# Block-sparse attention and its feed-forward on one core: the opening ordered by head, two score banks, spare matmuls further on, the last output in halves

## The chip, the cores and the metric

The kernel runs on 1 core of one Trainium2 chip. The metric is the device time of one execution in microseconds. The version before took 211.35 us as the median of 8 runs (210.47 to 214.65).

A core has TensorE (PE in the profile, its weight loads PEld), VectorE (DVE), ScalarE (ACT), GpSimd (POOL) and SyncE (SP, which here issues most transfers). Each runs its own instructions in order; semaphores make one wait for another. Matmuls write to PSUM, from which ScalarE and VectorE read.

## The reference

Four batches, 8 heads, 768 positions, head size 64. A block of 32 positions sees its neighbours, the first and the last block, and three drawn blocks; the first and last block see all.

```python
scores = scale * np.matmul(q, k.transpose(0, 1, 3, 2))
...
mask[qb * block:(qb + 1) * block, kb * block:(kb + 1) * block] = True
...
attn = softmax(np.where(mask, scores, -1e9))          # over the last axis
x = (attn @ v).transpose(0, 2, 1, 3).reshape(3072, 512)
h = x @ w_in                                          # 512 -> 1024
solu = h * softmax(h)
ln = (solu - mean(solu)) / np.sqrt(var(solu) + 1e-06) * g_ln
out = ln @ w_out                                      # 1024 -> 512
```

## The kernel before, in words

**Attention.** Heads go in pairs (`pr`, 4 of them), queries in three tiles of 256 (`t`). Keys and queries are turned into `kT` and `qT`, with the head's 64 values in the rows and 24 more rows below: for keys a one-hot of the block, for queries a row of the mask (0 or a large negative number). So one product of 88 rows gives masked scores. A unit (batch, tile, pair) has 12 products of 128 keys by 256 queries (L500), in three score groups of four, `n` = 0 to 2: group 0 is all of the pair's first head, group 1 half and half, group 2 the second head. A score group fills a pair of PSUM banks (`sbank`, three in all), and ScalarE takes its exponential (L511) to `ex`. Three value groups (L521, 8 products each) multiply by `va`, whose last column of ones gives the sum; VectorE divides (L532, L535) into `x`.

**Feed-forward.** For 128 rows at a time: `x` is transposed by a transfer (L565; the first and the last tile on TensorE, L551 and L555), the first product (`hmm`, L576, in four steps of two matmuls) fills a pair of banks, ScalarE takes the exponential with its sum (L585), VectorE multiplies (L589), centres (L593) and takes statistics (L596, L599), GpSimd works out the scale (L601 to L607), the result is transposed (L615 or L551, L555), and the second product (`outp`, L622, four steps) goes to one of two banks `mbank`. The scaled result goes by VectorE (L632) or, in the last three tiles, ScalarE (L635) to `ot`, and by L638 to memory. 24 such half tiles make the output.

**Banks.** Before, pool `sh` holds all three `sbank` pairs and serves the opening's transposes and the scores of batch 0, tiles 0 and 1 (and the last first products). All other scores take `s`, the first two pairs; first products take `h`, the third. The two `mbank` serve transposes, mask products, value sums and second products.

**The opening.** L316 builds masks on GpSimd; L341 transposes the one-hot on TensorE; L345 and L349 copy it out of the same bank on VectorE and ScalarE; L333 and L336 form the block mask, L354 multiplies it out to query rows, L361 copies these. L446 casts the first keys and queries, L464 transposes them, L472 copies them into `kT` and `qT`. L378 and L381 fill the extra columns of `kb` and `qb` for later pairs; L372 makes the latter. Spare matmuls on ones (L683) are written to the third pair of banks ahead of the first score.

**The order.** All work is a list of operations with an engine, an estimated duration, dependencies, pools they take from and a due time. `Plan.run` (L87) places them with a small model of the engines: always the operation that can start earliest, and among those the one that is due first. The tables `A`, `F`, `Q` and `SHIFT` hold due times of units, feed-forward tiles, preparations and kinds of operation. The planned starts only set the order in which each engine's instructions are written, and how many spare matmuls go into a planned gap:

```python
if o.eng == "PE" and o.start <= begin:
    for _ in range(max(0, int((o.start - idle) * SPARE / 0.107))):
        nc.tensor.matmul(flat(sbank[2])[:, 0:P], onesf, onesf, start=True, stop=True)
```

Of the kernel before, what the change touches and what calls it, by code (L numbers as in the profile page):

```python
# [11 lines left out]
ALU = mybir.AluOpType  # L12
# [10 lines left out]
def act_us(n, sbuf=False):  # L23
    return (n + 60 + (52 if sbuf else 0)) / 1200
# [130 lines left out]
def kernel(  # L155
# [33 lines left out]

    SPARE = 1.0  # L190
    NST, NKB, NEX, NX, NE, NSO, NSOT, NXT, NOT = 4, 3, 9, 6, 2, 3, 3, 2, 3
# [82 lines left out]
    def load(b, pr, which, hs=(0, 2)):  # L274
        src, dst, nm = {"k": (k, kst, "kst"), "q": (q, qst, "qst"), "v": (v, vst, "vst")}[which]
        o0 = stage.get((which, b, pr))
        o = op("SP", 0.5, lambda o: nc.sync.dma_start(  # L277
            out=dst[(o0 or o).slot][:, hs[0] : hs[1]].rearrange("p h c d -> p h (c d)"),
            in_=src[b, 2 * pr + hs[0] : 2 * pr + hs[1]].rearrange("h (p c) d -> p h (c d)", p=P)),
            due=-50 + 0.5 * len(loads), take=None if o0 else (nm, "dq") if b else nm,  # L280
            load=LOAD * (hs[1] - hs[0]) / 2, after=loads[-1:])
        if b:
            o.last_of.append((o, "dq"))
            o.held["dq"][0] = 1
        stage.setdefault((which, b, pr), o)
        stage[(which, b, pr, hs[1])] = o
        loads.append(o)
# [27 lines left out]
    def sel(t, us, fill, base, cm, pat, deps, cmp=ALU.is_ge):  # L315
# [3 lines left out]
    ohs = sel(oneh, 0.3, 0.0, 0, NCH, [[1, NCH], [-BLK, NB]], [oh1])  # L319
    ohs = sel(oneh, 0.3, 0.0, BLK - 1, -NCH, [[-1, NCH], [BLK, NB]], [ohs])  # L320
    mids = sel(ident, 0.3, 1.0, 0, 1, [[-1, P]], [mid, ohs], ALU.not_equal)
    io = op("POOL", 0.2, lambda o: nc.gpsimd.iota(kbi, pattern=[[1, NB]], base=0, channel_multiplier=0), [mids],
            due=-2194)

    stat = io
    for args in ((-NEG, 1, -1, [[1, NB]]), (-NEG, 1, 1, [[-1, NB]]), (0.0, -1, 1, [[0, NB]]),
                 (0.0, NB - 2, -1, [[0, NB]])):
        stat = sel(static, 0.16, *args, [stat, stz])
    for c in (0, NB - 1):
# [9 lines left out]
    def selq_tr(o):  # L339
        for c in range(NCH):  # L340
# [3 lines left out]
    sqt = op("PE", NCH * 0.056, selq_tr, [ohs, mids], due=-2190, take="m")  # L344
    sqs = op("DVE", 0.5, lambda o: nc.vector.tensor_copy(out=flat(selq), in_=bank(sqt, BF16)[0:NB, 0:S]), [sqt],  # L345
             due=-2189, last_of=[sqt])


    krow = [op("ACT", 0.7, lambda o: nc.scalar.copy(out=kT[0][D:DM, 0, 0, :], in_=bank(sqt, BF16)[0:NB, 0:S]),  # L349
               [sqt], due=-2189, last_of=[sqt]),  # L350
            op("DVE", 0.37, lambda o: nc.vector.tensor_copy(out=kT[0][D:DM, 0, 1, :], in_=flat(selq)), [sqs],
               due=-2079.6)]
    mps = lambda o: bank(o)[0:NB]
    mmq = [op("PE", (hi - lo) * 0.00043, lambda o, lo=lo, hi=hi: nc.tensor.matmul(  # L354
        mps(o)[:, 0 : hi - lo], maskq, flat(selq)[:, lo:hi], start=True, stop=True), [mq, sqs], due=due, take="m")
        for lo, hi, due in ((0, TW, -2088), (TW, S, -2079))]

    def qrow_op(eng, us, hh, lo, hi, src, deps, due, last_of=()):
        def f(o):
# [4 lines left out]
    qrow = {(0, 0): qrow_op("ACT", 0.38, 0, 0, TW, lambda: mps(mmq[0])[:, 0:TW], mmq[:1], -2087, mmq[:1]),  # L364
            (1, 0): qrow_op("DVE", 0.38, 1, 0, TW, lambda: mps(mmq[0])[:, 0:TW], mmq[:1], -2079.6, mmq[:1]),
            (0, 1): qrow_op("DVE", 0.65, 0, TW, S, lambda: mps(mmq[1])[:, 0 : S - TW], mmq[1:], -2078, mmq[1:])}
    qrow[(1, 1)] = qrow_op("DVE", 0.3, 1, TW, S, lambda: qT[0][D:DM, 0, 0, TW:S], [qrow[(0, 1)]], -2077)
# [44 lines left out]
    def prepare(b, pr, due):  # L412
# [4 lines left out]
        for nm, st, cb, dst in (("k", kst, kb, kT), ("q", qst, qb, qT)):  # L417
# [23 lines left out]
            for part in range(2):  # L441
                due_ = (-2085, -2080)[part] if first else due

                def cast(o, st=st, cb=cb, ld=ld, c0=cas[0] if cas else None, hs=slice(part, part + 1 if first else 2)):
                    d_, s_ = cb[(c0 or o).slot][:, hs, :, 0:D], st[ld.slot][:, hs]
                    (nc.scalar.copy if o.eng == "ACT" else nc.vector.tensor_copy)(out=d_, in_=s_)  # L446

                e = "ACT" if first and nm == "q" else "DVE"
                n = S // 2 if first else S
                if first or not part:  # L450
                    cas.append(op(e, act_us(n, True) + 0.1 if e == "ACT" else dve_us(n, 2), cast,
                                  [stage[(nm, b, pr, part + 1 if first else 2)]], due=due_,
                                  take=None if cas else nm + "b", last_of=[ld], after=cas[:1]))
            ca = cas[0]
            for hh in range(2):
                due_ = (-2085, -2080)[hh] if first else due
                rows = D if first else DM

                where = "sh" if first and hh == 0 else "m"
                at = pair16 if where == "sh" else lambda o: bank(o, BF16)  # L460

# [7 lines left out]
                for lo, hi in ((0, TW), (TW, S)) if first and nm == "q" else ((0, S),):  # L469
                    def cp(o, dst=dst, hh=hh, t=t, rows=rows, lo=lo, hi=hi, at=at):  # L470
# [3 lines left out]
                    e2 = "ACT" if first and nm == "q" and hh == 0 and lo == 0 else "DVE"  # L474
                    x = op(e2, act_us(hi - lo) if e2 == "ACT" else dve_us(hi - lo, 2) + 0.07, cp, [t],
                           due=-2078 if lo else due_ + 0.1, last_of=[t])
                    if first and nm == "q":
# [12 lines left out]
    def attend(b, t, pr, A):  # L490
# [4 lines left out]
        for n in range(3):  # L495
            def score(o, n=n):
                s = sbank[o.slot]
                for m in range(4):
# [4 lines left out]

            so = op("PE", 4 * 0.1087, score, need[0] + (need[1] if n else []), due=A + 0.9 * n,
                    take="sh" if b == 0 and t < 2 else "s")
            last_use.setdefault((b, pr), []).append(so)
# [51 lines left out]
    def feed(b, t, F, by_pe, late):  # L558
# [10 lines left out]
        for a in range(2):  # L569
# [44 lines left out]
            else:  # L614
                st = op("SP", xbar_us(64), lambda o, so=so: nc.sync.dma_start_transpose(  # L615
                    out=sotb[o.slot], in_=sob[so.slot]), [ce] + wo, due=F[a] - 200, take="soT", load=64 * TILE,
                        last_of=[so])
            o0 = None
            for n in range(4):
                def outp(o, n=n, o0=o0, st=st):  # L620
                    for f in (2 * n, 2 * n + 1):
                        nc.tensor.matmul(bank(o0 or o), sotb[st.slot][:, f, :], w_out_sb[:, f, :],  # L622
                                         start=(f == 0), stop=(f == KF - 1))

                om = op("PE", 2 * 0.2156, outp, [st] + wo, due=F[a] + 7 + 0.8 * n, take=None if n else "m",
                        last_of=[st] if n == 3 else [], after=[om_last] if n else [])
                o0 = o0 or om
                om_last = om

            def fin(o, o0=o0, rs=rs):  # L630
                if o.eng == "DVE":
                    nc.vector.tensor_scalar(out=otb[o.slot], in0=bank(o0), scalar1=rsb[rs.slot],  # L632
                                            scalar2=None, op0=ALU.mult)
                else:
                    nc.scalar.activation(out=otb[o.slot], in_=bank(o0), func=ACT.Copy, scale=rsb[rs.slot])  # L635

            fo = op("ACT" if late else "DVE", 0.52 if late else 0.74, fin, [om, rs], due=F[a] + 7, take="ot", last_of=[o0, rs])
            op("SP", 0.45, lambda o, a=a, fo=fo: nc.sync.dma_start(  # L638
                out=out_v[b, 2 * t + a], in_=otb[fo.slot]), [fo], due=F[a], last_of=[fo], load=0.8)

# [3 lines left out]

    A = [51.93, 316.63, -115.93, 231.11, 59.19, -252.77, -562.27, -274.63, -180.24, 25.80, 75.07, -201.10,
         -31.34, -93.78, 23.73, -319.92, -93.53, -52.89, -80.83, -22.04, -376.92, -9.75, 205.17, 275.41,
         -112.76, -464.51, -631.08, -498.27, -7.06, -372.28, 157.83, 217.60, 84.04, 320.33, 507.35, 414.39,
         21.67, -219.75, 54.16, 178.38, -53.69, 42.58, -611.35, 171.75, -151.43, -138.86, 342.15, 543.94]
    F = [-197.56, -107.72, -104.30, -8.09, -3.95, 17.64, 606.07, -83.42, 40.06, 52.29, -182.87, 23.22, -123.31,
         -316.31, -64.31, 252.67, -96.19, 36.13, 1165.15, 493.27, 30.32, 16.50, -322.54, 402.30]  # L650
    Q = [-885.18, -425.71, -91.22, 353.64, 159.27, 116.44, -98.95, 40.67, 1195.36, 573.14, 90.68, 27.21,
         212.02, 207.45, 1374.23, 1441.29]
    for b in range(B):
# [15 lines left out]

    SHIFT = {"score": 83.14, "hmm": 360.52, "outp": 460.27, "pv": -613.9}  # L670
    for o in plan.ops:
# [4 lines left out]

    begin = min(o.start for o in order if o.emit.__name__ == "score")
    idle = m1.seen
    with tc.manual_schedule():
        for o in order:  # L680
            if o.eng == "PE" and o.start <= begin:
                for _ in range(max(0, int((o.start - idle) * SPARE / 0.107))):
                    nc.tensor.matmul(flat(sbank[2])[:, 0:P], onesf, onesf, start=True, stop=True)  # L683
                idle = o.start + o.us * (2 if o.start < COLD else 1)
            o.emit(o)
# [30 lines left out]
```

## Time and profile before

| | |
|---|---|
| median of 8 runs | 211.35 us (210.47 to 214.65) |
| the profiled execution | 210.63 us, span 208.9 us |
| TensorE granted clock, mean | 0.997 |
| exponentials of scores (L511) | 144, 137.6 us busy, 1040 ns each |
| score products (L500) | 576, 82.8 us busy, 272 ns each |
| value products (L521) | 1152, 43.1 us busy, 193 ns each |
| first products (L576) | 192, 51.3 us busy |
| second products (L622) | 192, 47.7 us busy |
| spare matmuls (L683) | 26, 3.1 us busy |

Matmuls overlap, so the mean of one holds its way through the array; the pace is read from start times. ScalarE's exponentials overlap a little too. A group's "idle before" is time in which its engine stood still, with what ended it. "8.61 33.65 ... x36" in a timeline is a row of merged instructions: start, length, number.

### The profile page before, as it was taken

What the parts mean: (1) busy time and instruction counts of PE and PEld (TensorE: products, weight loads), DVE (VectorE), ACT (ScalarE), POOL (GpSimd) and SP (SyncE); (2) the same over time, 40 slices, a digit from 0 to 9 for tenths busy, and PEclk for the clock granted to TensorE, in tenths of its full rate; (3) what the DMA queues carried; (4) which work ended last, traced back from release to release, by engine and by line L of the source; (5) the groups of instructions that cost most, each with busy time, mean ns of one, the idle gap of its engine ahead of it and who ended that gap; (6) DMA issues with size and microseconds to landing.
All of it is one profiled execution on the core that took longest, in us unless ns stands there. A gap on an engine that the chain in (4) does not pass through costs nothing.

```text
span 208.9 us, 5807 instructions
## 1 busy us (share of the span) xinstructions
PE 199.8 (96%) x2298; PEld 141.2 (68%) x2298; DVE 158.1 (76%) x373; ACT 169.9 (81%) x208; POOL 63.0 (30%) x131
## 2 busy tenths in 40 slices
PE   7899998989999999999999999999999999999991
PEld 6689887767769676877776677666676755664540
DVE  3898979849988657767768775988887496889960
ACT  6699999998999999989989689886989837745331
POOL 5143034305631013623325523363210111311140
PEclk9999999999999999999999999999999999999998
DMA  5999998999984186999999999999790464634522
GB/s 171 325 383 349 265 322 176 197 245 261 248 112 111 29 204 226 275 168 292 177 211 234 291 124 320 188 359 202 174 196 3 104 151 110 143 86 118 152 104 100
DMA packets 69120, 41.28 MB, mean 198 GB/s; under 512 B 52189, under 2 KB 64485, under 8 KB 69093
## 3 DMA queue, kind: packets, MB, share of 16 engines
q1 hardware_dynamic: 68496, 39.86, 77.4%
q0 software_dynamic: 544, 1.05, 2.6%
q8 instruction: 18, 0.29, 0.6%
q14 instruction: 10, 0.07, 0.1%
q10 hardware_dynamic: 52, 0.00, 0.0%
HBM read 23.07 MB, written 6.29 MB: 141 GB/s over the span
## 4 chain that ended last, share of the span: by engine, by line
PE 80%; ACT 11%; DVE 3%; DMA 2%; issue 1%; SPq 1%; ACTq 0%
PE sbank L500 25%; PE mbank L622 20%; PE sbank L576 18%; PE mbank L521 14%; ACT ex L511 9%; DMA qst<-in_q_dram 2%; PE mbank L464 2%; PE mbank L551 1%; ACT eso L585 1%; DVE qb L381 1%; SPq L277 1%; DVE eso L589 1%; DVE eso L593 0%; DVE kb L446 0%; DVE kT L432 0%
## 5 line engine op out<-in xcount | busy, mean ns | idle before, releaser
L511 ACT ACTIVATE ex<-sbank 128x1024 bf16<-128x1024 f32 x144 | 137.6, 1040 | 10.4 <-PE sbank L500 9.7
L500 PE MATMUL sbank<-qT,kT 88*128 88x256 bf16 x576 | 82.8, 272 | 2.6 <-ACT ex L511 1.9
L500 PEld LDWEIGHTS <-kT 88*128 88x128 bf16 x576 | 52.5, 97 | 24.2 <-issue 5.7
L576 PE MATMUL sbank<-w_in_sb,xT 128*128 128x512 bf16 x192 | 51.3, 379 | 0.0
L622 PE MATMUL mbank<-w_out_sb,eso 128*128 128x512 bf16 x192 | 47.7, 379 | 0.0
L521 PEld LDWEIGHTS <-ex 128*128 128x128 bf16 x1152 | 41.7, 97 | 5.2 <-issue 0.3
L521 PE MATMUL mbank<-va,ex 128*128 128x65 bf16 x1152 | 43.1, 193 | 0.1
L585 ACT ACTIVATE eso<-sbank 128x1024 bf16<-128x1024 f32 x24 | 24.8, 1033 | 15.0 <-PE sbank L576 10.5
L589 DVE SCALAR_TENSOR_TENSOR eso<-sbank,eso 128x1024 bf16<-128x1024 f32 x24 | 29.3, 1220 | 10.1 <-ACT eso L585 10.0
L596 DVE BATCH_NORM_STATS2 bn<-eso 128x6 f32<-128x512 bf16 x48 | 30.7, 680 | 0.2
L622 PEld LDWEIGHTS <-eso 128*128 128x128 bf16 x192 | 18.4, 98 | 17.1 <-DVE eso L555 0.5
L576 PEld LDWEIGHTS <-xT 128*128 128x128 bf16 x192 | 18.6, 98 | 11.2
L603 POOL TENSOR_SCALAR mv<-se,mv 128x1 f32<-128x1 f32 x24 | 7.2, 300 | 61.3 <-DVE mv L599 52.0
L532 DVE RECIPROCAL r<-mbank 128x4 f32<-128x4 f32 x48 | 8.2, 175 | 20.6 <-PE mbank L521 20.2
L535 DVE TENSOR_TENSOR x<-mbank,r 128x256 bf16<-128x256 f32 x48 | 19.8, 417 | 0.8
L482 POOL CAST va<-vst 128x768 bf16<-128x768 f32 x16 | 13.8, 863 | 17.5 <-DMA vst<-in_v_dram 14.5
L632 DVE TENSOR_SCALAR ot<-mbank,rs 128x512 f32<-128x512 f32 x18 | 13.5, 748 | 4.0 <-PE mbank L622 3.4
L422 POOL CAST kb<-kst 128x768 bf16<-128x768 f32 x12 | 10.4, 863 | 15.9 <-DMA kst<-in_k_dram 15.2
L607 POOL TENSOR_TENSOR rs<-mv,neg_half 128x1 f32<-128x1 f32 x24 | 13.5, 563 | 5.2 <-DVE ot L632 3.9
L601 POOL TENSOR_TENSOR se<-se 128x1 f32<-128x1 f32 x24 | 4.8, 200 | 32.1 <-ACT eso L585 32.1
L593 DVE TENSOR_SCALAR eso<-eso,mu 128x1024 bf16<-128x1024 bf16 x24 | 12.7, 529 | 0.3
L422 POOL CAST qb<-qst 128x768 bf16<-128x768 f32 x12 | 10.1, 839 | 7.5 <-DMA qst<-in_q_dram 3.7
(73 smaller groups left out, 108.4 us busy)
## 6 DMA issues: line engine op xcount, KB each, us to landing
vst<-in_v_dram SPq DMA_DIRECT2D x16, 384.0 KB, 4.4
out_dram<-ot SPq DMA_DIRECT2D x24, 256.0 KB, 2.4
kst<-in_k_dram SPq DMA_DIRECT2D x15, 384.0 KB, 5.3
qst<-in_q_dram SPq DMA_DIRECT2D x15, 384.0 KB, 6.3
w_in_sb<-in_moe_w_in_dram POOLq DMA_DIRECT2D x2, 512.0 KB, 11.3
kT<-in_moe_w_out_dram SPq DMA_DIRECT2D x1, 768.0 KB
qT<-in_moe_w_out_dram SPq DMA_DIRECT2D x1, 768.0 KB, 14.6
eso<-in_moe_w_out_dram SPq DMA_DIRECT2D x1, 512.0 KB
```

What stands on the lines that cost most here:

```text
L422: nc.gpsimd.tensor_copy(out=half(cb[o.slot], 0).rearrange("p (c h d) -> p c h d", c=NCH, h=2), in_=st[ld.slot].rearrange("p h c d -> p c h ...
L482: vc = op("POOL", pool_us(S) + 0.3, lambda o: nc.gpsimd.tensor_copy(out=va[i][:, 2 * pr : 2 * pr + 2, :, 0:D], in_=vst[ld.slot]), [ld, von ...
L500: nc.tensor.matmul(s[:, m, :], kT[i][0:DM, pr, hh, jc * P : (jc + 1) * P], qT[i][0:DM, pr, hh, t * TW : (t + 1) * TW], start=(m % 2 == 0), ...
L511: exs.append(op("ACT", act_us(1024), lambda o, so=so: nc.scalar.activation(out=exb[o.slot], in_=sbank[so.slot], func=ACT.Exp, scale=scale) ...
L521: nc.tensor.matmul(acc[:, qt, hh, :], exb[exs[n].slot][:, m, qt * P : (qt + 1) * P], va[i][:, 2 * pr + hh, jc, :], start=(n + m + qt == 0) ...
L535: nrm = op("DVE", 0.41, lambda o: nc.vector.tensor_tensor(out=xb[x_of[(b, t)].slot][:, :, 2 * pr * D : (2 * pr + 2) * D].rearrange("p a (h ...
L576: nc.tensor.matmul(h[:, f * 512 : (f + 1) * 512], xTb[xp.slot][:, a, c, :], w_in_sb[:, c, f * 512 : (f + 1) * 512], start=(c == 0), stop=( ...
L585: se = op("ACT", act_us(d_ff) + 0.22, lambda o, h0=h0: nc.scalar.activation(out=eb[o.slots["e"]], in_=pair(h0), func=ACT.Exp, accum_out=se ...
L589: so = op("DVE", 1.3, lambda o, h0=h0, se=se: nc.vector.scalar_tensor_tensor(out=sob[o.slot], in0=pair(h0), scalar=1.0, in1=eb[se.slots["e ...
L596: bn = op("DVE", 2 * 0.68, lambda o, so=so: [nc.vector.bn_stats(out=bnb[o.slot][:, f], in_=sob[so.slot][:, f * 512 : (f + 1) * 512]) for f ...
L607: rs = op("POOL", 0.55, lambda o, mv=mv: nc.gpsimd.tensor_tensor(out=rsb[o.slot], in0=mvb[mv.slot][:, 0:1], in1=neg_half, op=ALU.pow), [q2 ...
L622: nc.tensor.matmul(bank(o0 or o), sotb[st.slot][:, f, :], w_out_sb[:, f, :], start=(f == 0), stop=(f == KF - 1))
```

## The change

- The opening's operations get other engines and due times. The one-hot rows go from PSUM to `selq` by ScalarE (not VectorE), and VectorE makes both copies into `kT` from `selq` in SBUF (before: ScalarE from the bank, VectorE from `selq`). The second head's query cast goes to VectorE. The second mask product comes earlier. ScalarE's fills of `kb` come after the first query cast.
- Where two engines copied parts out of one bank, the second now depends on the first (`first_x`, and `qrow[(1, 0)]` on `qrow[(0, 0)]`).
- Scores of batch 0 and the opening's transposes take the two pairs of pool `s`; the third pair is left to spare matmuls until the first product of the feed-forward.
- Spare matmuls go into planned gaps up to the first `hmm` (before: up to the first score), at 0.9 of the gap, counted at 0.0535 us once the planned time is past `COLD`.
- Some estimates in the planner's model change, among them the loads' and GpSimd's.
- The second product of the very last tile is made in two halves of 256 columns, each in its own bank; the first is scaled by VectorE, the second by ScalarE, and each is sent on its own.
- New tables `A`, `F`, `Q`, `SHIFT` (all numbers differ).

Every engine's order from there on is the planner's, and differs through the whole kernel: on TensorE the first scores now go group 0 of tiles 0, 1 and 2, then group 1 of tile 0; value groups often stand one or two at a time between scores; the first feed-forward product stands after 30 score groups (before: after 36). There are 66 spare matmuls (before 26).

```diff
-    SPARE = 1.0
+    SPARE = 0.9
...
-    sqs = op("DVE", 0.5, lambda o: nc.vector.tensor_copy(out=flat(selq), in_=bank(sqt, BF16)[0:NB, 0:S]), [sqt],
+    sqs = op("ACT", 0.75, lambda o: nc.scalar.copy(out=flat(selq), in_=bank(sqt, BF16)[0:NB, 0:S]), [sqt],
              due=-2189, last_of=[sqt])
-    krow = [op("ACT", 0.7, lambda o: nc.scalar.copy(out=kT[0][D:DM, 0, 0, :], in_=bank(sqt, BF16)[0:NB, 0:S]),
-               [sqt], due=-2189, last_of=[sqt]),
-            op("DVE", 0.37, lambda o: nc.vector.tensor_copy(out=kT[0][D:DM, 0, 1, :], in_=flat(selq)), [sqs],
-               due=-2079.6)]
+    krow = [op("DVE", 0.36, lambda o, hh=hh: nc.vector.tensor_copy(out=kT[0][D:DM, 0, hh, :], in_=flat(selq)), [sqs],
+               due=(-2087.5, -2079.8)[hh]) for hh in range(2)]
...
-        for lo, hi, due in ((0, TW, -2088), (TW, S, -2079))]
+        for lo, hi, due in ((0, TW, -2088), (TW, S, -2084.6))]
...
+    qrow[(1, 0)] = qrow_op("DVE", 0.4, 1, 0, TW, lambda: mps(mmq[0])[:, 0:TW], [mmq[0], qrow[(0, 0)]], -2079.6, mmq[:1])
...
-                e = "ACT" if first and nm == "q" else "DVE"
+                e = "ACT" if first and nm == "q" and part == 0 else "DVE"
...
+                    if e == "ACT":
+                        for f in filled["k"]:
+                            plan.follow(f, cas[0])
...
-                where = "sh" if first and hh == 0 else "m"
+                where = "s" if first and hh == 0 else "m"
...
-                    x = op(e2, act_us(hi - lo) if e2 == "ACT" else dve_us(hi - lo, 2) + 0.07, cp, [t],
-                           due=-2078 if lo else due_ + 0.1, last_of=[t])
+                    x = op(e2, act_us(hi - lo) if e2 == "ACT" else dve_us(hi - lo, 2) + 0.07, cp, [t, first_x],
+                           due=due_ + 0.1 + (0.4 if lo else 0), last_of=[t])
+                    first_x = x
...
-                    take="sh" if b == 0 and t < 2 else "s")
+                    take="s")
...
+            w = d_model // 2 if by_pe and late and a else d_model
+            for col in range(0, d_model, w):
...
+                            nc.tensor.matmul(bank(o0 or o)[:, 0:w], sotb[st.slot][:, f, :],
+                                             w_out_sb[:, f, col : col + w], start=(f == 0), stop=(f == KF - 1))
...
+                e = "ACT" if late and not (col == 0 and w < d_model) else "DVE"
...
-    SHIFT = {"score": 83.14, "hmm": 360.52, "outp": 460.27, "pv": -613.9}
+    SHIFT = {"score": -128.51, "hmm": 94.0, "outp": 390.35, "pv": -23.13}
...
-    begin = min(o.start for o in order if o.emit.__name__ == "score")
+    begin = min(o.start for o in order if o.emit.__name__ == "hmm")
...
-                for _ in range(max(0, int((o.start - idle) * SPARE / 0.107))):
+                for _ in range(max(0, int((o.start - idle) * SPARE / (0.107 if o.start < COLD else 0.0535)))):
```

## The prediction

> **What bounds the kernel now.** I read the page first, then the stretches, the two engines' timelines, the opening row by row and the chain of waits at the end.
>
> ```profile
> PE 199.8 (96%) x2298; PEld 141.2 (68%) x2298; DVE 158.1 (76%) x373; ACT 169.9 (81%) x208; POOL 63.0 (30%) x131
> ...
> PEclk9999999999999999999999999999999999999998
> ...
> 8.60:42.50 33.90, 32.48 (x503) 27.71 (x503) 29.43 (x70) 33.52 (x37) 10.22 (x12) 1.00 1.03 283
> 42.50:60.00 17.50, 16.36 (x206) 12.06 (x205) 14.73 (x33) 16.48 (x20) 8.11 (x13) 1.00 1.02 227
> 60.00:186.00 126.00, 125.45 (x1434) 87.25 (x1431) 94.30 (x225) 106.52 (x130) 36.35 (x75) 1.00 0.80 183
> ```
>
> The last three lines are stretches (busy us of PE, PEld, DVE, ACT, POOL, then clock, DMA share, GB/s). Up to 42.5 ScalarE is the full engine (33.52 of 33.90); from 60 on it is TensorE (125.45 of 126). So an opening that is shorter, or exponentials that come faster, bring the end forward only by what TensorE gets done earlier. The granted clock is 1.00 in each stretch.
>
> ```profile
> 8.61 33.65 ACT L511 ACTIVATE ex<-sbank 128x1024 bf16<-128x1024 f32 x36 [1.19 <-PE sbank L500]
> 42.47 1.96 ACT L511 ACTIVATE ex<-sbank 128x1024 bf16<-128x1024 f32 x2 [0.21 <-PE sbank L500]
> ```
>
> 36 exponentials (exps) without a break: (33.65 - 1.02) / 35 = 0.93 us each, against 0.905 when nothing is late (three from 56.71 take 2.85). This is with three score banks. The next view is a later stretch, where the scores have two, as they have in the changed kernel from the start.
>
> ```profile
> 60.42 7.89 ACT L511 ACTIVATE ex<-sbank 128x1024 bf16<-128x1024 f32 x8
> ...
> 62.45 0.60 PE L500 MATMUL sbank<-qT,kT 88*128 88x256 bf16 x4
> 62.88 0.91 PE L521 MATMUL mbank<-va,ex 128*128 128x65 bf16 x24
> 63.63 0.60 PE L500 MATMUL sbank<-qT,kT 88*128 88x256 bf16 x4
> ```
>
> Here the pace is (7.89 - 1.02) / 7 = 0.98. A score group (0.44 us on TensorE by its start times) and a whole triple of value groups (0.75) take 1.18 between two scores, 0.28 more than one exp. With two banks an exp (1.02 until its bank is free), the start of the next score (0.06 to 0.08: 56.81 to 56.87) and score to exp (0.70: 55.09 to 55.79) make 1.80, which is twice 0.90: nothing is left over.
>
> ```profile
> 3.46 0.55 DVE L345 COPY selq<-mbank 24x768 bf16<-24x768 bf16 x1 [0.55 <-PE mbank L341]
> 4.04 0.79 ACT L349 COPY kT<-mbank 24x768 bf16<-24x768 bf16 x1
> 4.85 0.51 ACT L446 CAST qb<-qst 128x384 bf16<-128x384 f32 x1
> 4.86 0.85 PE L464 MATMUL sbank<-ident,kb 128*64 128x128 bf16 x6
> 6.00 0.52 PE L464 MATMUL sbank<-ident,qb 128*64 128x128 bf16 x6
> 7.05 0.36 ACT L472 COPY qT<-sbank 64x256 bf16<-64x256 bf16 x1
> 7.53 0.49 PE L464 MATMUL mbank<-ident,qb 128*64 128x128 bf16 x6 [0.68 <-DVE qT L361]
> ```
>
> The opening. The first score starts at 7.96, right behind the second head's query transposes (7.53), though ScalarE had its inputs ready at 7.41.
>
> ```profile
> 201.90 2.77 PE mbank L622 x12
> 204.67 0.03 ACTq L635
> 204.70 0.05 issue
> 204.75 0.69 ACT ot L635
> ```
>
> The end of the chain: last matmul to 204.67, copy to 205.44, transfer, span 208.9.
>
> **The change, part by part**, against the profiled execution's 210.63 us (0.72 under the median of 211.35; its span is 208.9).
>
> *Opening, first exp.* The copy of the selection rows goes to ScalarE (0.79 there, 3.46 to 4.25), and the 0.79 copy that stood at 4.04 goes to DVE from SBUF (0.35, after it). The query cast then starts at 4.25 to 4.6 (its load's landing is not shown; it was there by 4.85) instead of 4.85. The three mask fills of kb wait behind that cast, on ScalarE, where nothing is due until the query copies. On DVE the key cast comes first, and TensorE has 7 spares ahead of the key transposes and not 13 (1.57 / 13 each), so these start at 4.2 to 4.6, not 4.86. Query transposes: about 5.3, not 6.00. Then ScalarE's two copies (0.36 each) to about 6.9 and the score at 7.1; exp 0.65 later (as 7.96 to 8.61): 7.9, **-0.7**. Bounds -0.3 (the loads land late) and -1.1.
>
> *Opening, exps 2 to 8.* The order by head gives three score groups that need only head 0, but each waits for DVE: key copy 0.55, key cast 0.36, query copy 0.42 (it now waits for ScalarE's copy out of the same bank; the old trace had those in sequence too: 7.41, then 7.51), mask row 0.68. That ends at 8.0. The key transposes of head 1 stand ahead of the second score on TensorE and wait for that mask row's bank: score 8.4, exp 9.1 (before: 9.53). Then on DVE: query cast of head 1 (0.36, moved here from ScalarE), rows 0.42 and 0.28, key copy 0.54, query copy 0.27, cast of the next pair 0.55, query copy 0.41, three mask copies of 0.46 to 12.1; TensorE's transposes for the next pair wait for the last of these (one bank of two). I get exp 8 at 15.1, as before (15.09). So the 0.7 is **given back, +0.7**; bounds 0 and +1.0.
>
> *Exps 9 to 36 on two banks.* Before, from exp 8 to the 37th, 27.4 us. In the changed kernel's order on TensorE, between the 9th and 31st scores, I count between two scores: five whole triples (0.28 each over one exp), triple plus transposes (0.62), two value groups plus transposes (0.37), two transposes (0.20) and three small ones (0.13): 2.7 us. 29 exps at 0.905 are 26.2. One feed-forward exp now comes before the 37th (1.0 on ScalarE); it covers the 0.8 over that I count from the 31st on. 26.2 + 2.7 + 1.0 = 29.9: **+2.5**. Bounds: +0.5 (only the feed-forward exp less half a us) and +3.
>
> *Spares.* 66 against 26; 20 stand ahead of the first score, the other 46 between it and the first feed-forward group, 0.056 each by the rows after 6 us, 2.6 us in all, in runs of at most 6 (0.34). ScalarE sets the pace there; a run stands in a gap that TensorE would wait through. Taken as 0; where a gap isn't there, each run delays a score, at most 2.6. A gain is excluded, as the clock is 1.00 already. The Trainium skill ("TensorE: Matmul & The Clock Gate", Part 1) says that the array's clock falls only after an idle window of some 3.4 us; the longest wait of TensorE after 8 us is 1.03, so by it, too, the spares in the gaps are worth 0, and if it were wrong the trace would show a clock under 1.00 somewhere.
>
> *Work done earlier.* When score 37 starts, the changed kernel has done 5 feed-forward pairs and not 2; all else is equal in number (33 value groups, 16 transposes, 1 x-transpose). 3 pairs of 0.43: **-1.3** off what is left.
>
> *After score 37.* What is left before is 108 scores x 0.436, 111 value groups x 0.25, 94 + 96 pairs x 0.432, 5 transposes x 0.45 = 159.2; it took 204.67 - 41.8 = 162.9, so 3.7 were waits and matmul floors, 1.14 of them between 42.5 and 60. With first products and first outputs 3 to 5 pairs ahead I take these 1.1 as gone: **-1.1**; bounds 0 and -2. Late next would be the transfers: the channel is full (1.02 to 1.03) and SP's order has one xT transpose and the second query transpose earlier, the qst load later. The old kernel's batch-1 rows waited 0.3 on DVE at 40.5; scores are now 2 us later, so 0. GpSimd's order is the same up to there.
>
> *Last output in halves.* 16 matmuls of 256 columns for 8 of 512: 1.74 for 1.73. The copy that ends last is 256 wide: 0.36 for 0.69, -0.33. The transfer is half as big: -0.1 (0 to -0.5: the loads of 192 and 384 KB land in 3.0 and 5.3 us, on a full channel). The second half waits for a bank that DVE reads (0.74) while the first half (0.87) runs: +0.2. **-0.25**. DVE has three sums and statistics in a row there: bounds -0.6, +0.9.
>
> Sum: -0.7 + 0.7 + 2.5 - 1.3 - 1.1 - 0.25 = -0.15: **210.5 us**.
>
> **The rivals.**
> *Faster: the order covers the triples.* If ScalarE runs on two banks as it did on three, the +2.5 shrinks to the 1.0 of the feed-forward exp, and DVE doesn't give the 0.7 back: -0.7 + 1.0 - 1.3 - 1.1 - 0.25 = -2.35, 208.3. For it: steps of 0.90 occur on two banks wherever nothing over 0.47 stands between scores, and here value groups are often single. Against: 0.98 in the fence above.
> *Slower: the lost bank is not made good.* The same +2.5, work in hand -1.3, but none of the 1.1 comes back and DVE holds the last tiles (+0.9): +2.1, 212.7. It decides from an exp pace over 0.98 in the first 36. For it: DVE is 29.43 of 33.90 busy there.
> *Slower: the clock is released later.* Transposes go at 107 ns until 5.5 us and at 56 from 6.08, after spares almost without a gap. With 17 spares and not 26 by then (10 and 7), the release may miss; at 107 the first three scores and four transposes cost 3 x 0.44 + 4 x 0.3, about 2.5 less what waits anyway: +2, 212.6.
> *The change does nothing that lasts:* opening hidden, 210.6; that lies in the forecast's own range.
>
> **How the numbers follow.** Forecast 0.46 (own range 209.0 to 212.2), covered triples 0.31, lost bank 0.15, late clock 0.08. One per cent (2.1 us) is about what a measurement of this kernel can tell from no change. Over 1% faster is most of the second case and the forecast's edge: 0.28; slower the last two: 0.24; within 0.48. The range 208.0 to 213.0 reaches into the cases on both sides.
>
> **What would show it.** First exp near 7.9 with 56 ns transposes from about 6; eighth step near 15; the pace of the first 36 exps 0.99 to 1.02; the 37th score exp near 45; TensorE without a wait over 0.5 from 46 on; the last copy 0.36. Wrong if that pace stays at 0.93 (then 208.3), or if transposes are still at 107 at 7 us.

## The result, and the profile after

The changed kernel takes 210.18 us (median of 24 executions, 209.08 to 214.45) against 211.16 us before (64 executions, 210.04 to 214.65, over all the comparisons). The ratio is 0.9941, interval [0.9927, 0.9956]: 1.2 us less, inside the 1% that the prediction called no change. The forecast of 210.5 was worked out from the old profiled execution: 0.15 less was expected there, and the profiled executions differ by 0.91 (210.63 to 209.72, spans 208.9 and 208.0). A part of the executions of nearly every version here, before and after too, is 3 to 5 us longer and left out of the ratios, so where there were six executions the ratio is to be read and not the median.

By the start times of the two profiled executions:

| mark, us | before | after | difference | predicted |
|---|---|---|---|---|
| first exp | 8.61 | 6.69 | -1.92 | -0.7 |
| 8th exp | 15.09 | 14.12 | -0.97 | 0 |
| 37th score exp | 42.47 | 44.07 | +1.60 | +2.5 |
| last matmul ends | 204.66 | 204.60 | -0.06 | +0.3 |
| last copy ends | 205.43 | 205.24 | -0.20 | 0.0 |
| span | 208.86 | 207.98 | -0.88 | -0.15 |

The steps between the marks say more than the sum: up to the 8th exp the opening brought 1 us that was not forecast, the stretch on two banks cost what was forecast (+2.58), the way from there to the last matmul gave back 1.67 and not 2.2, and the end behind the last matmul 0.8 and not 0.43.

The page of the kernel after, its busy times and the granted clock in 40 slices:

```profile
PE 200.9 (97%) x2346; PEld 144.2 (69%) x2346; DVE 158.2 (76%) x375; ACT 169.7 (82%) x207; POOL 63.3 (30%) x131
...
PEclk9999999999999999999999999999999999999999
```

The stretches of the kernel after, cut where its own first and 37th exps lie (busy us of PE, PEld, DVE, ACT, POOL, clock, DMA share, GB/s):

```profile
6.69:44.07 37.38, 36.44 (x566) 31.77 (x566) 33.43 (x75) 35.55 (x38) 12.08 (x14) 1.00 0.93 277
44.07:60.00 15.93, 15.93 (x176) 11.42 (x175) 13.03 (x32) 14.91 (x19) 7.89 (x13) 1.00 1.14 260
60.00:186.00 126.00, 125.92 (x1468) 88.40 (x1466) 92.80 (x226) 108.42 (x132) 35.56 (x74) 1.00 0.81 183
```

In the first stretch ScalarE is now busy for 35.55 of 37.38 us: 1.8 us of gaps where it had 0.4 of 33.90. TensorE's 36.44 there includes the 46 later spares, so it says little. From 44 on TensorE has no gap left (15.93 of 15.93, 125.92 of 126), where it had 1.14 and 0.55: that part of the forecast holds.

The opening of the kernel after, TensorE's timeline (start, length; "x6" are six matmuls in a row; L341 transposes the one-hot, L695 are spares, L466 the transposes of keys and queries, L503 scores):

```profile
2.33 0.80 PE L341 MATMUL mbank<-ident,oneh 128*24 128x128 bf16 x6
3.06 0.93 PE L695 MATMUL sbank<-onesf 128*128 128x128 bf16 x7
3.91 0.76 PE L466 MATMUL sbank<-ident,kb 128*64 128x128 bf16 x6
4.50 0.50 PE L466 MATMUL sbank<-ident,qb 128*64 128x128 bf16 x6
...
6.06 0.60 PE L503 MATMUL sbank<-qT,kT 88*128 88x256 bf16 x4 [0.36 <-ACT qT L359]
6.88 0.49 PE L466 MATMUL mbank<-ident,kb 128*64 128x128 bf16 x6 [0.22 <-DVE qT L359]
```

The key transposes start 0.95 earlier than the old row at 4.86, the query transposes 1.50 earlier than the one at 6.00, and they already take 0.50 for six: in this execution the pitch of matmuls falls from 107 to 56 ns at about 4.4 us (before: between 5.5 and 6.1). The two last rows hold the waits that hand part of it back: the first score waits 0.36 for ScalarE's copy of head 0's mask row, and the second head's key transposes wait 0.22 for the bank from which VectorE copies the rest of that row.

ScalarE's timeline of the kernel after, at the first exps and at the first one of the feed-forward:

```profile
6.69 1.02 ACT L514 ACTIVATE ex<-sbank 128x1024 bf16<-128x1024 f32 x1 [0.69 <-PE sbank L503]
7.95 8.24 ACT L514 ACTIVATE ex<-sbank 128x1024 bf16<-128x1024 f32 x8 [0.24 <-PE sbank L503]
...
33.47 5.83 ACT L514 ACTIVATE ex<-sbank 128x1024 bf16<-128x1024 f32 x6 [0.49 <-PE sbank L503]
39.45 1.02 ACT L514 ACTIVATE ex<-sbank 128x1024 bf16<-128x1024 f32 x1
40.37 1.02 ACT L588 ACTIVATE eso<-sbank 128x1024 bf16<-128x1024 f32 x1
```

Eight exps in 8.24 us are (8.24 - 1.02) / 7 = 1.03 us each, against 0.93 before; the feed-forward exp at 40.37 (before: 44.32) is the 1.0 us that the prediction put ahead of the 37th.

The end, TensorE's timeline of the kernel after:

```profile
192.38 1.46 PE L629 MATMUL mbank<-w_out_sb,eso 128*128 128x512 bf16 x6
194.61 5.34 PE L629 MATMUL mbank<-w_out_sb,eso 128*128 128x512 bf16 x24 [0.78 <-ACT ot L643]
199.79 0.61 PE L554 MATMUL mbank<-ident,eso 128*128 128x128 bf16 x8
200.78 3.82 PE L629 MATMUL mbank<-w_out_sb,eso 128*128 128x512 bf16 x24 [0.38 <-ACT ot L643]
```

and of the kernel before:

```profile
194.68 1.89 PE L576 MATMUL sbank<-w_in_sb,xT 128*128 128x512 bf16 x8
196.41 0.61 PE L551 MATMUL mbank<-ident,eso 128*128 128x128 bf16 x8
196.85 4.48 PE L622 MATMUL mbank<-w_out_sb,eso 128*128 128x512 bf16 x20
201.30 0.61 PE L551 MATMUL mbank<-ident,eso 128*128 128x128 bf16 x8
201.74 2.92 PE L622 MATMUL mbank<-w_out_sb,eso 128*128 128x512 bf16 x12
```

L629 is the second product (L622 before), L554 the transposes (L551), L643 ScalarE's scaled copy of the output (L635). Before, first products (L576) stood among the last outputs, and no row waits. After, the first products are done by 191.5; what is left all goes through the two `mbank`, and the transposes L554 hold one of them: 0.78 and 0.38 of waits on ScalarE's output copy. The chain of waits of the kernel after ends so:

```profile
203.56 1.05 PE mbank L629 x8
204.61 0.03 ACTq L643
...
204.76 0.47 ACT ot L643
```

The last copy, of 256 columns, takes 0.47; predicted was 0.36.

### The profile page after: what moved, and what is told of

It is laid out like the page before. It is cut to its first block, busy times and chain, and to the rows that moved or that the text cites. A ratio compares the mean times of both kernels' runs of the same rounds, so it can differ in the third digit from the quotient of the medians.

```text
span 208.0 us, 5910 instructions
## 1 busy us (share of the span) xinstructions
PE 200.9 (97%) x2346; PEld 144.2 (69%) x2346; DVE 158.2 (76%) x375; ACT 169.7 (82%) x207; POOL 63.3 (30%) x131
## 4 chain that ended last, share of the span: by engine, by line
PE 86%; ACT 7%; DVE 3%; issue 1%; ACTq 0%
PE sbank L503 27%; PE mbank L629 20%; PE sbank L579 19%; PE mbank L524 16%; ACT ex L514 5%; PE mbank L466 2%; PE mbank L554 1%; PE sbank L695 1%; ACT ot L643 1%; DVE qT L359 1%; ACT L271 1%; DVE kT L474 1%; ACT eso L588 0%; DVE w_out_sb L401 0%; DVE qT L474 0%
## 5 line engine op out<-in xcount | busy, mean ns | idle before, releaser
L503 PE MATMUL sbank<-qT,kT 88*128 88x256 bf16 x576 | 85.0, 272 | 0.8 <-ACT qT L359 0.4
L503 PEld LDWEIGHTS <-kT 88*128 88x128 bf16 x576 | 52.5, 97 | 23.6 <-issue 3.3
L629 PE MATMUL mbank<-w_out_sb,eso 128*128 128x512 bf16 (+1 forms) x200 | 48.7, 370 | 1.2 <-ACT ot L643 1.2
L524 PEld LDWEIGHTS <-ex 128*128 128x128 bf16 x1152 | 45.0, 97 | 5.2 <-DVE x L538 0.4
L524 PE MATMUL mbank<-va,ex 128*128 128x65 bf16 x1152 | 47.2, 193 | 0.3 <-DVE x L538 0.3
L629 PEld LDWEIGHTS <-eso 128*128 128x128 bf16 x200 | 18.5, 97 | 15.7 <-issue 2.0
L579 PEld LDWEIGHTS <-xT 128*128 128x128 bf16 x192 | 17.8, 98 | 10.7
L640 DVE TENSOR_SCALAR ot<-mbank,rs 128x512 f32<-128x512 f32 (+1 forms) x19 | 14.0, 734 | 8.0 <-POOL rs L610 3.9
L643 ACT ACTIVATE ot<-mbank,rs 128x512 f32<-128x512 f32 (+1 forms) x6 | 3.9, 651 | 10.9 <-PE mbank L629 9.8
L596 DVE TENSOR_SCALAR eso<-eso,mu 128x1024 bf16<-128x1024 bf16 x24 | 11.9, 498 | 0.1
```

What stands on the lines that cost most here:

```text
L503: nc.tensor.matmul(s[:, m, :], kT[i][0:DM, pr, hh, jc * P : (jc + 1) * P], qT[i][0:DM, pr, hh, t * TW : (t + 1) * TW], start=(m % 2 == 0), ...
L524: nc.tensor.matmul(acc[:, qt, hh, :], exb[exs[n].slot][:, m, qt * P : (qt + 1) * P], va[i][:, 2 * pr + hh, jc, :], start=(n + m + qt == 0) ...
L579: nc.tensor.matmul(h[:, f * 512 : (f + 1) * 512], xTb[xp.slot][:, a, c, :], w_in_sb[:, c, f * 512 : (f + 1) * 512], start=(c == 0), stop=( ...
L629: nc.tensor.matmul(bank(o0 or o)[:, 0:w], sotb[st.slot][:, f, :], w_out_sb[:, f, col : col + w], start=(f == 0), stop=(f == KF - 1))
L640: nc.vector.tensor_scalar(out=otb[o.slot][:, 0:w], in0=bank(o0)[:, 0:w], scalar1=rsb[rs.slot], scalar2=None, op0=ALU.mult)
```

## The experiments

Marks are read from each kernel's trace, ratios are against the kernel before, run beside it; for the kernel after it is 0.9941.

**The opening and its spares.** Two kernels change the spare matmuls of the kernel after: one puts 16 more ahead of the first score, the other has none at all.

```diff
+                more = 16 if o is first else 0
-                for _ in range(max(0, int((o.start - idle) * SPARE / ...))):
+                for _ in range(more + max(0, int((o.start - idle) * SPARE / ...))):
```

> The changed kernel with 16 more spare matmuls directly ahead of the first score; nothing else moves. 16 of them take 0.9 us at 56 ns, some 0.35 of it in the wait that TensorE has there anyway (0.36 at 6.06). Theory (the opening is on the path, since ScalarE is full from the first exponential until TensorE is): first exponential 0.5 to 0.6 later, eighth and 37th as much later, the end 0.4 to 0.7 later. Rival 1 (VectorE's chain paces exponentials 2 to 8): first later, eighth within 0.15 of 14.12, the end unchanged. Rival 2 (the busier array releases or holds the clock otherwise): the 56 ns pitch starts at another time than 4.4 us and decides.

Ratio 0.997 [0.9926, 1.0014]: 0.6 us more than after by the middle values, with overlapping intervals. Its profiled execution held 107 ns until about 10 us, as the second rival has it; the first exp stands at 9.50 (+2.8 on after), the 8th at 16.65 (+2.5), the 37th at 47.33 and the last matmul's end at 207.86 (+3.26 each). In this execution nothing of the time lost in the opening comes back. It took 212.96 us, though, and six of the nine executions in the ratio took 209.32 to 209.94, about 0.993 of the kernel before and so no longer than after. So the theory's 0.4 to 0.7 for the 16 spares themselves doesn't show, and that a shift by the order alone arrives at the end whole is not shown either.

```diff
-    SPARE = 0.9
+    SPARE = 0.0
```

> The changed kernel without any spare matmul, order kept. Theory (the 20 at the start are what gets the clock released before the first score, the other 46 nothing): 107 ns per 128 columns until 8 us or later, first exponential 0.5 to 1.0 us later than 6.69, the eighth 1 to 4 later, and the time 1 to 4 us longer. Rival (the opening's own transposes release the clock as well): within 0.5 us of the changed kernel.

Ratio 1.0073 [1.0047, 1.0098], 2.8 us more than after; all 12 executions lie between 211.88 and 213.37. TensorE's timeline of the kernel without spares:

```profile
4.42 0.85 PE L466 MATMUL sbank<-ident,qb 128*64 128x128 bf16 x6
...
15.25 1.06 PE L503 MATMUL sbank<-qT,kT 88*128 88x256 bf16 x4
16.10 0.85 PE L466 MATMUL mbank<-ident,qb 128*88 128x128 bf16 x6
16.74 0.78 PE L503 MATMUL sbank<-qT,kT 88*128 88x256 bf16 x4
...
18.10 0.60 PE L503 MATMUL sbank<-qT,kT 88*128 88x256 bf16 x4
```

Four score matmuls take 1.06 until 16 us and 0.60 from 18. The first exp is late by only 0.46 (7.15), the 8th by 3.4 (17.55), and 3.1 of it is still there at the last matmul. This kernel lacks the later spares too; against the one below, which lacks only those (1.0003), the 20 of the opening are worth 0.007, some 1.5 us, and the pitch shows how: an opening in the new order, but cold, loses more than the 1 us that the opening brought.

**The spares after the first score.** The kernel after with its 46 later spares left out, in the same order:

```diff
-    begin = min(o.start for o in order if o.emit.__name__ == "hmm")
+    begin = min(o.start for o in order if o.emit.__name__ == "score")
```

> The changed kernel with its order kept, without the 46 spare matmuls that stand between the first score and the first feed-forward product (the 20 ahead of the first score stay). Theory (they stand in gaps that TensorE waits through anyway, and the clock needs none of them): the time of the changed kernel within 0.4 us, granted clock 1.00 in every stretch, the 37th score exponential within 0.3 of 44.07. Rival 1 (they keep the clock up): the clock or the 56 ns pitch is lost somewhere before 40 us, and the time rises by 1 us or more. Rival 2 (they delay scores): up to 2.6 us faster, the pace of the first 36 exponentials falls from 1.03 towards 0.93.

Ratio 1.0003 [0.9971, 1.0035], 1.3 us above after; the theory had 0.4 at most. The pitch fell to 56 ns at 4.4 us as in after and stayed there, so the clock is not what they hold here. Two things differ in the trace: the 37th exp is at 44.71 (+0.64), and the last wait of the end changes its releaser. TensorE's timeline of this kernel:

```profile
195.25 5.34 PE L629 MATMUL mbank<-w_out_sb,eso 128*128 128x512 bf16 x24 [0.78 <-ACT ot L643]
200.43 0.61 PE L554 MATMUL mbank<-ident,eso 128*128 128x128 bf16 x8
202.08 3.83 PE L629 MATMUL mbank<-w_out_sb,eso 128*128 128x512 bf16 x24 [1.04 <-DMA eso<-eso]
```

1.04 for a transfer that lands late stands where after has 0.38 for a bank. Why a transfer 150 us later should depend on these spares is not settled. The kernels below that leave them out change the banks as well, so they don't settle it.

**The third bank.** First the other way round: the kernel before with its first 30 score groups on two banks, order kept.

```diff
+    for n, o in enumerate([o for o in order if o.emit.__name__ == "score"][:30]):
+        o.slots[o.take[0]] = n % 2
```

> The kernel before with its order kept, but its first 30 score groups take two pairs of banks in turn and not three. Theory (two banks leave no room for a triple between two scores): between the first score and the 37th I count 5.5 us over one exponential's time, where three banks let 1.1 through, so the 37th exponential comes 2.5 to 4.4 us later than 42.47, and the end, with the work left the same, 2 to 4 us later: 213 to 215 in the profiled execution. Rival (the third pair was worth little, since VectorE's copies set the pace in both): later by less than 0.7 us.

In this kernel some exponentials read another group's scores, as they are written after the score group that takes their bank. Ratio 1.024 [1.0199, 1.0282]. It settles nothing on the bank's price, because the clock was lost as well. The stretches of this kernel:

```profile
4.00:8.00 4.00, 2.26 (x28) 1.82 (x27) 2.06 (x8) 2.80 (x6) 0.20 (x1) 0.98 0.97 295
8.00:12.00 4.00, 3.82 (x23) 2.02 (x23) 2.54 (x7) 1.62 (x3) 0.85 (x2) 0.50 1.03 374
12.00:18.00 6.00, 5.73 (x48) 4.26 (x46) 4.93 (x12) 3.60 (x5) 3.17 (x4) 0.50 1.07 379
```

There is a wait of 1.6 us at 6.6 (the second head's query transposes, on VectorE), TensorE is busy for 2.26 of 4 us, and the granted clock is 0.50 for the next ten. The pitch was 56 ns from 4.5 us to that wait, and 107 behind it.

Then the kernel after, without later spares (they are written to the third pair) and with three banks for its first 27 score groups:

```diff
+    for n, o in enumerate([o for o in order if o.emit.__name__ == "score"][:27]):
+        o.slots["s"] = n % 3
```

> The same without the late spares, and the first 27 score groups take the three pairs of banks in turn; the order of every engine is kept. Theory (the lost third pair costs ScalarE about 2.5 us over the first 36 exponentials, and this goes on to the end because TensorE is full from there): the 37th exponential comes 1.5 to 2.5 us earlier than in the changed kernel (44.07), at 41.6 to 42.6, and the time falls by 1.2 to 2.2 us against it, to some 207.7 to 208.7 in the profiled execution. Rival 1 (VectorE's chain of casts and copies holds the transposes, not the banks): the pace stays at 1.0 or more and the time changes by less than 0.5. Rival 2 (what comes earlier waits later, for the batch-1 rows or the first product's weights): the exponentials come earlier by as much, the end by less than 0.7.

Ratio 0.9949 [0.9912, 0.9987]: 1.1 us less than the same kernel on two banks (1.0003), by middle values whose intervals overlap; 1.2 to 2.2 were expected. Its profiled execution had 107 ns until 16 us, so its marks can't be set beside those of after; a combined kernel, below, gives them.

**A bank for the last transposes.** The kernel after, where the last two transposes of the feed-forward write to a score bank, idle by then, and the last outputs take the two `mbank` in turn:

```diff
-        t = mbank[o.slot]
+        t = sbank[o.pair].rearrange("p a b -> p (a b)")[:, 0:512] if hasattr(o, "pair") else mbank[o.slot]
...
+    trs = [o for o in order if o.emit.__name__ == "tr"][-2:]
+    for o in trs:
+        o.pair = 1
...
+    for n, o in enumerate(last):
+        o.slots["m"] = (n + 1) % 2
```

> The changed kernel, its order kept, with the last two groups of transposes (those of the two tiles that TensorE transposes itself at the end) in a pair of score banks, which is free by then; the second products of the end then take the two other banks by turns and none waits for ScalarE's copy of the one before. Theory (TensorE's two waits at the end, 0.78 at 194.61 and 0.38 at 200.78, come from the transposes holding one of two banks): the time falls by 0.8 to 1.2 us against the changed kernel. Rival (behind the bank stands the transfer that transposes the last tile but one, which lands at about 200.5 whatever TensorE does): it falls by less than 0.3, and the wait shows up as one for that transfer.

> The same kernel as the one with the last two transposes on TensorE in a score bank, run again, because its first profile had its opening at 107 ns a matmul until 16 us and can't be set beside the other traces. Tail theory (the two waits of 0.78 and 0.38 on one of two mbanks cost the end 1.3 us): ratio to before 0.985 to 0.989, last feed-forward exp to last matmul 11.3 to 11.6 us against 12.84. Rival (the tail gain was chance of the six runs): ratio 0.992 to 0.996.

Ratios 0.9864 [0.9814, 0.9914] and 0.9857 [0.9819, 0.9896]: 1.6 and 1.8 us less than after, more than the 0.8 to 1.2 first expected. From the start of the last feed-forward exp to the last matmul's end it is 11.36 us in both traces, against 12.84 in after. TensorE's timeline of the second run:

```profile
191.88 6.64 PE L629 MATMUL mbank<-w_out_sb,eso 128*128 128x512 bf16 x30
198.35 0.61 PE L554 MATMUL sbank<-ident,eso 128*128 128x128 bf16 x8
198.80 3.82 PE L629 MATMUL mbank<-w_out_sb,eso 128*128 128x512 bf16 x24
```

No row waits for the transposes' bank. The 1.48 are the two waits by start times: in after, 192.38 to 194.61 less six matmuls of 0.216 is 0.94, and 199.79 to 200.78 less eight transposes of 0.056 is 0.54 (the view counts them, as 0.78 and 0.38, from the modelled ends of the matmuls ahead). The rival of the second run, that the first gain was chance, falls. So does that of the first, a transfer that lands late: no row waits for one here.

**Both, twice.** Three score banks, no later spares, and the bank for the transposes:

> The same, and also without the 46 late spares and with three pairs of banks for the first 27 score groups. Theory (two banks cost 2.5 us over the first 36 exponentials): 37th exponential at 41.6 to 42.6 where the array's clock is released as in the changed kernel, and the time 1.2 to 2.2 us under the same kernel with two banks: 2.0 to 3.4 us under the changed kernel. Rival 1 (VectorE's copies hold the opening): 37th exponential after 43.5, gain only that of the end. Rival 2 (an earlier first product waits for its weights or the batch-1 rows): 37th exponential as the theory has it, the 49th less than 1 us earlier than 58.6.

> The third score bank for the first 27 score groups, no late spares, and the tail bank, run again for an interval beside the tail-bank version. Theory (the third bank is worth 0.9 to 1.5 us at the 37th score exp): ratio lower than the tail-bank version's by 0.004 to 0.007, at 0.979 to 0.983. Rival (what the third bank gains is given back by TensorE further on): the two within 0.002.

Ratios 0.9832 [0.9769, 0.9894] and 0.9848 [0.981, 0.9887]; the shortest execution is 207.43 us. It beats both kernels. Against the tail-bank version beside it, it is 0.0032 and 0.0009 lower, within the intervals: the second was expected at 0.004 to 0.007, and the rival's "within 0.002" is what came. ScalarE's waits from 10 to 60 us (in total, times, longest), first in the kernel after:

```profile
ACT ex L514 <- PE sbank L503: 1.8, 7, 0.5
```

then in the first of these two:

```profile
ACT ex L514 <- PE sbank L503: 1.5, 6, 0.3
```

and in the second run of the tail-bank version, on two banks:

```profile
ACT ex L514 <- PE sbank L503: 1.2, 5, 0.3
```

These waits don't tell two banks from three. By the marks of the first (opening as in after: first exp 6.71, 8th 14.43), 8th to 37th takes 28.73 us; on two banks it is 29.95 in after, 29.59 in the tail-bank version, 30.53 without later spares. One pair alone doesn't give the bank's price: over all profiles in this order the stretch takes 29.56 to 30.69 on two banks (eight of them) and 28.73, 29.02 and 29.60 on three, and the means differ by 0.8. The 37th at 43.16 also misses the theory's 41.6 to 42.6. The tail-bank version has its 8th exp 0.43 earlier (14.00), so at the 37th the three banks are 0.43 ahead (43.16 against 43.59), and at the last matmul 0.23 (202.39 against 202.62). TensorE has no gap from 44 on in after, so exps that come sooner would find it busy; that this is where the other 0.2 went is argued, not shown.

**The last output whole.** First the kernel after, then the tail-bank version, with the last output in one piece:

```diff
-            w = d_model // 2 if by_pe and late and a else d_model
+            w = d_model
```

> The changed kernel with the last output whole, as before: 8 matmuls of 512, one copy, one transfer; nothing else moves. Theory of the result (the halves bring 0.2 on the copy and 0.7 on what follows it: from the last copy's end to the end of the span 2.8 us with halves and 3.5 without): slower than the changed kernel by 0.7 to 1.0 us. The prediction's term: slower by 0.25. Rival (the shorter end came from elsewhere, the last transfer alone in its queue): 0.0 to 0.3.

> The tail-bank version with the last output whole instead of in halves. Theory of the prediction (halves worth 0.25 us: copy 0.33 and transfer 0.1 less, a bank wait of 0.2 more): 0.4 us slower than the tail-bank version beside it, as its bank wait is gone too, ratio higher by 0.002; last copy 0.69 and not 0.47. Rival (the transfer's half is worth more, 0.7 to 1.0 as the spans of the first profiles had it): ratio higher by 0.0035 to 0.005.

Ratios 0.9955 [0.9935, 0.9976] against after's 0.9941 (0.3 us), and 0.9893 [0.9843, 0.9942] against 0.9857 (0.8 us, from two executions); the intervals overlap both times. The rows are finer than the ratios. Whole, in the first of these kernels, the copy ends 0.77 after the last matmul, in halves (after) 0.64; last copy to the end of the span takes 3.11 against 2.75; but TensorE needs 12.63 and not 12.84 from the last feed-forward exp on. The tail-bank pair gives the same within 0.01. In sum 0.3 for the halves. The transfers' issues in the last 8 us of the kernel after (count, KB each, median us to landing):

```profile
out_dram<-ot SPq DMA_DIRECT2D x2, 256.0 KB, 2.1
out_dram<-ot SPq DMA_DIRECT2D x2, 128.0 KB, 1.7
```

Half the bytes land 0.4 sooner (0.36 by the spans); the forecast had 0.1.

## Why the prediction was right or wrong, by its own steps

*Opening, first exp: -0.7 forecast, -1.92 measured; outside the bounds.* The mechanism was right (selection rows on ScalarE, key cast first, fewer spares ahead), its size wrong in each link: ScalarE's copy starts at 3.16 and not 3.46, as three spares fewer stand ahead of the one-hot transposes; the query cast at 3.85 and not 4.25 to 4.6; the transposes run at 56 ns from 4.4. That the release comes with less matmul time behind it than before is the opposite of the late-clock rival. In part this is luck: in four of the nine profiles with this opening the pitch of 107 ns lasts to 16 us or longer (see the last section).

*Exps 2 to 8: +0.7 forecast, +0.95 measured.* VectorE takes back what it was said to take, within its bounds. With the first exp so early that leaves -0.97 and not 0. That such a shift reaches the end whole is shown for a late clock only: the two runs of the tail-bank version are 4.36 apart at the 8th exp and 4.37 at the last matmul.

*Exps 9 to 36 on two banks: +2.5 forecast, +2.58 measured* (29.95 for 29.9). The forecast charged no separate price to the bank; it counted matmul blocks between scores, at 0.905 an exp. Of the +2.58, 1.0 is the feed-forward exp that comes earlier; the lost bank is 1.2 by the three-bank run (28.73, no later spares) and 0.8 by the means above, and the rest, 0.4 to 0.8, is put down to the order, which no run separates. With a spread of 1.1 us among the two-bank profiles, the hit to 0.1 is closer than the forecast could be; its 0.905, too, is 0.915 by its own three exps in 2.85 ((2.85 - 1.02) / 2), which over 29 exps would add 0.3. "Covered triples" at 208.3 did not come; the tail-bank version, with executions from 207.72, is near it by another way.

*Spares: 0 forecast.* They slow nothing that can be seen. But "a gain is excluded, as the clock is 1.00 already" is not borne out as it stands: without the later ones the kernel was 1.3 us slower, with the clock at 1.00 throughout. The cause of this is open.

*Work done earlier -1.3 and waits after score 37 -1.1: -1.67 measured for both*, with the +0.2 of the last bank wait in it. The step that failed is the second. From 44 to 186 TensorE has indeed lost its waits (0.1 us of gaps, where it had 1.7 from 42.5 on); the forecast then took the end as it was, but there TensorE lost 1.48 to waits on `mbank`, where before no row waits. The prediction had named first products that run ahead as the gain and not asked what stays behind for the end: only work on two banks. The tail-bank runs show this as the cause. The forecast of -2.2 with the 1.48 added would be -0.72; of the 0.95 between that and -1.67, 0.5 are the waits behind 60, which went too (0.55 to 0.08), and 0.5 stay open.

*Last output in halves: -0.25 forecast, 0.3 measured by the pairs with and without.* Its terms: copy -0.33 became -0.13, transfer -0.1 became -0.4, the bank wait +0.2 is 0.2 by start times, and it stays in the tail-bank version. Behind the last matmul the end is 0.8 shorter than before; the halves make 0.5 of it (copy and transfer), and the other 0.3 comes from elsewhere: last copy to the end of the span is 3.43 before and 3.11 with the same whole transfer in the kernel after. That 0.3 isn't explained.

The total was near by luck, because misses partly cancelled: of the 0.75 between -0.9 and -0.15, the opening makes -1.0, the two banks +0.1, the rest of the way +0.5 and the end -0.4.

The lost-bank rival (212.7) had its decisive sign in the trace: the pace of the first 36 exps, (44.07 - 6.69) / 36 = 1.04, lies over 0.98, and over the forecast's own 0.99 to 1.02. But the forecast has that sign too. The rival failed elsewhere: it had the opening at 0 (measured -1.0), only -1.3 behind score 37 (-1.67), and +0.9 at the end (-0.8). "TensorE without a wait over 0.5 from 46 on" held up to 194.

## What to carry to other kernels

When an order lets one kind of work run ahead, look at what that leaves for the end, and which buffers this alone can use: here two banks that were enough in the mix became the bound, and an idle bank of another pool took 1.5 us off. What a local gain is worth is read at the end: the third score bank gained some 0.8 us in its stretch, and at the end between 0.2 (beside the tail-bank version) and 1.1 (beside the kernel without later spares), neither of them clear of the noise. And an opening's order is to be judged together with the clock: without any spares the kernel lost 2.8 us, and a clock that was released late cost one and the same kernel 4.4 us at the last matmul.

## What the runs showed of the hardware

- The pitch of 107 ns ends at very different times in executions of the same opening: 4.4 us in after, between 5.1 and 5.5 in the second tail-bank run, 16.4 in the first, which runs the same instructions up to there. Of the nine profiles with this opening's 20 spares, five have it end by 5.5 us and four at 16 to 18. In the first tail-bank run TensorE was busy for 8.00 of 8.00 us from 4 to 12 (the first busy number of each row), and its last matmul ends 4.4 us later (206.99 against 202.62):

```profile
4.00:8.00 4.00, 4.00 (x27) 2.64 (x27) 3.74 (x9) 2.62 (x7) 0.93 (x2) 1.00 0.98 326
8.00:12.00 4.00, 4.00 (x29) 2.46 (x28) 2.92 (x8) 2.34 (x3) 0.83 (x1) 1.00 1.06 385
```

  The Trainium skill ("TensorE: Matmul & The Clock Gate", Part 1) says that full speed comes after a busy window of some 3.4 us and that the window runs freely. That the time differs between executions agrees; that 8 us of full busy time, more than two such windows, did not release it does not.
- The clock can be lost behind a short wait: in the kernel before on two banks the pitch went from 56 to 107 ns behind one wait of 1.60 us. The 3.4 us of idle time that the prediction took as the bound does not hold in that execution. The wait of 1.03 us in the kernel before cost nothing of the kind: four score matmuls behind it took 0.60.
- The record of the granted clock does not always show it: it stood at 1.00 in every stretch of the kernel without spares up to 18 us, while four score matmuls took 1.06 and not 0.60; in the kernel before on two banks it stood at 0.50 when they took 1.03. The pitch of the matmuls is the safer sign. The same page warns that these records are unreliable, which agrees.
- A transfer of 128 KB to memory landed in 1.7 us and one of 256 KB in 2.1 (medians of two each). Estimated from these two, with time taken as a fixed part and one in proportion to size, 1.3 us do not depend on the size. The Trainium skill ("DMA: Bandwidth & Descriptors", "Anatomy of one DMA") gives about 2.0 us as the fixed part, on GpSimd's path; these go by SyncE's queue, and the whole of the smaller one is below that.
